# Sixteen small tiles instead of four in the products with P and dS of a recurrent attention kernel

## The chip, the cores and the metric

The kernel runs on one core of a Trainium2 chip. The metric is device time of one execution in microseconds. A core has TensorE (PE, matrix products, with its weight loads shown apart as PEld), VectorE (DVE), ScalarE (ACT), GpSimd (POOL) and SyncE (SP, which issues most transfers). PE writes into PSUM, eight banks of 2 KB in each of 128 partitions, from where DVE and ACT copy ("evict") results to SBUF. A matmul can be placed on a part of the 128x128 array: `tile_position=(r, c)` puts it on the rows from r and the columns from c. Its rows are the partitions that it reads, its columns the PSUM partitions that it writes.

## The reference

A training step, forward and backward, of a layer with two branches over 2048 tokens of width 512: `x + A(xn) + B(xn)`, with xn the layer norm of x. Branch B is a squared-ReLU MLP. Branch A goes through 64 segments of 32 tokens, with 32 heads of width 128 and 8 memory rows:

```python
for s in range(n_seg):
    h = jnp.concatenate([mem, xs], axis=1)          # 8 + 32 rows
    q = jnp.einsum('btd,dhe->bhte', h, Wq)          # and k, v
    p = _softmax(where(mask, scores, -1e9))
    o = einsum(einsum(p, v), Wo)
    mem = o[:, :M, :]                               # goes into the next segment
...
_out, _vjp = jax.vjp(_f, A_x, A_mem0, A_Wq, ...)
```

Outputs are the layer's output and the gradients of all inputs and weights. The memory rows make the segments a serial chain, forward in one direction and backward in the other.

## The kernel before

The program has four stages. The first (0 to about 250 us) is the layer norm and branch B. The second is the forward recurrence (to about 1300 us), the third the backward recurrence (to about 2515 us), the last accumulates the weight gradients of branch A and the layer norm's gradient.

In both recurrences one segment is one call of `chain(s)`, and four segments make a block of 128 tokens. The 32 heads lie in 4 groups of 32 partitions by 8 slots: tile [128, 8, 128], partition group j, slot i, head 4i + j. A projection (`proj`, lines 407 to 421) puts four heads' columns on four column groups of the array at once and evicts in two halves of four slots. `to_T` transposes 128x128 pieces on PE.

In the forward, `chain` (line 907) does q and k, their transposes, scores, softmax on DVE and ACT, transposes P in 32x32 squares on DVE, and then `diag` (line 441) multiplies P with V for each head: out (32 x 128) = P (32 x 32 or 32 x 8, the weights) times V (32 x 128), two terms (own rows and memory rows). As a head's P and V lie in partition group j and its output shall lie there as well, `diag` uses the four tiles on the diagonal of the array, tile_position (32j, 32j), one half of four slots into one PSUM bank, 32 matmuls a half. Each half is evicted with its own copy of 128x512 (`evict`), transposed on DVE in 32x32 squares (`sq_T`, 128x512) and multiplied with Wo (`wo_part`, line 814), 128 matmuls, whose result gives the next segment's memory.

In the backward, `chain` (line 1236) does the projection gO, its transposes gOT, dP = gO V^T (line 1249), the softmax's gradient on DVE (`smax_bwd`, lines 1101 to 1106, four operations), which gives dS, and three `diag` products: part 2 (P with gO), part 1 (dS with q) and part 0 (dS transposed with k). Each is evicted, transposed by `sq_T` and goes through `dh_part` (line 1117, 64 matmuls of 512 columns) into one PSUM bank. That bank is copied to R_A, summed over the groups (gm, line 1284) and written into the next segment's input (line 1287).

Other blocks' work fills the gaps: in the forward the weight gradients of branch B (`dw_unit`, line 1009) and the four memory-row sets of a block in one go (`l_proj`, `l_attn`, names with L); in the backward `l_pre` and `l_post`, with an own `diag` each (oL and dqL), and in `l_post` two products `own` (line 1194) and `mm` (line 1205) that add up in one bank per half.

The order is made by a planner (`_Plan`): every piece of work is added with a cost in us for the engines that can do it, with what it reads and writes. `run()` simulates with these costs and issues the pieces in the order found, so that each engine's queue has a fixed order. PE work has a shape ("d" for diag, "w" for column groups, "f" for the whole array), and a turn between shapes costs 0.095 us in the plan.

PSUM banks come from pools of the tile framework. In the forward kinds c, f and m have 4, 2 and 2 banks (`NBK`), in the backward c, r and f have 5, 1 and 2. `Stage.bank` gives the banks of a kind in turn.

## Time and profile before

| | us |
|---|---|
| median of 3 runs | 3122.26 (3120.48 to 3124.76) |
| profiled execution: span | 3097.7 |
| PE busy in the span | 2792.6 |
| DVE busy | 1538.8 |
| ACT busy | 933.7 |
| forward recurrence, one segment (250 to 1300, 64 segments) | 16.4 |
| backward recurrence, one segment (1369 to 2515) | 17.9 |

The span is counted from the first to the last instruction of the profiled execution. The runs time the whole execution: their median is 24.6 us above the span. In the lines of the profile, "x" counts instructions, "idle before" is the time in which an engine stood still ahead of an instruction, and the name behind the arrow is what ended it. "issue" stands for time in which the engine waited for nothing that the profile shows. Busy time of PE is modelled and counts overlapping matmuls once.

### The profile page before, as it was taken

Reading aid. Unit: us, or ns where it says so; the run is one execution under the profiler, and the core shown is the slowest. Engines: PE = TensorE matmul, PEld = TensorE weight load, DVE = VectorE, ACT = ScalarE, POOL = GpSimd, SP = SyncE. Lnnn points to the kernel's source line nnn. Section 1 sums busy time; section 2 is a strip of 40 time slices with the busy share of each in tenths; the row PEclk is TensorE's granted clock in tenths of the full one; section 3 lists DMA queues with packets and bytes.
Section 4 is the critical chain, followed back from the end, with each engine's and each line's share of the span. In section 5 each row is a group of like instructions: output and inputs, shape, how many; then the busy total and the mean of one; then the engine's idle time right before and its main releaser. Section 6 shows DMA issues by size and latency. Waiting matters only on the chain.

```text
span 3097.7 us, 138545 instructions
## 1 busy us (share of the span) xinstructions
PE 2792.6 (90%) x62681; PEld 1629.5 (53%) x62847; DVE 1538.8 (50%) x3390; ACT 933.7 (30%) x1809; POOL 260.8 (8%) x434
## 2 busy tenths in 40 slices
PE   8998889898889898798888898889899889999999
PEld 6664555555555555564555555555555544444444
DVE  5544545555545455575555565565556521233322
ACT  4323434433434344342233333333333310000000
POOL 1110000000000000100000000000000001121111
PEclk9999999999999999999999999999999989999999
DMA  6647655566665563357677777777777669789861
GB/s 205 217 155 212 173 157 171 160 174 167 163 160 153 162 168 125 98 143 195 184 208 193 204 204 202 207 200 213 208 214 206 201 238 351 223 253 280 253 184 45
DMA packets 554918, 590.54 MB, mean 191 GB/s; under 512 B 250197, under 2 KB 355110, under 8 KB 552150
## 3 DMA queue, kind: packets, MB, share of 16 engines
q1 hardware_dynamic: 538758, 527.06, 59.8%
q0 software_dynamic: 15568, 54.61, 5.3%
q8 instruction: 491, 8.04, 1.2%
q14 instruction: 101, 0.83, 0.1%
HBM read 283.32 MB, written 262.68 MB: 176 GB/s over the span
## 4 chain that ended last, share of the span: by engine, by line
PE 67%; issue 10%; DVE 8%; DMA 8%; SPq 3%; ACT 2%; POOL 1%; ACTq 0%; POOLq 0%; DVEq 0%
PE ps_gw L1448 11%; PE ps_dRA L1117 9%; PE ps_d L451 6%; PE ps_RA L814 4%; PE ps_q L415 4%; PE ps_k L415 3%; PE ps_h L609 3%; PE ps_gO L415 3%; SPq L361 3%; PE ps_dRL L1117 3%; PE ps_v L415 2%; PE ps_dw L1009 2%; PE ps_gm L1284 2%; PE ps_o L451 2%; PE ps_gxb L637 2%
## 5 line engine op out<-in xcount | busy, mean ns | idle before, releaser
L1117 PE MATMUL ps_dRA<-WA,dT 128*32 128x512 bf16 x6144 | 376.6, 385 | 12.9 <-issue 10.4
L1448 PE MATMUL ps_gw<-WA,WB 128*128 128x512 bf16 x1505 | 330.7, 379 | 2.2 <-DVE gwo L316 0.6
L415 PEld LDWEIGHTS <-PA 128*32 128x32 bf16 x8192 | 207.5, 98 | 235.7 <-issue 29.8
L1448 PEld LDWEIGHTS <-WB 128*128 128x128 bf16 x1896 | 185.4, 98 | 225.0 <-issue 1.9
L399 DVE STREAM_TRANSPOSE dT<-dN 128x512 bf16<-128x512 bf16 x384 | 255.5, 692 | 90.7 <-ACT dN L318 89.4
L318 ACT CAST dN<-ps_d 128x512 bf16<-128x512 f32 x356 | 198.8, 588 | 292.0 <-PE ps_d L451 257.2
L1117 PEld LDWEIGHTS <-dT 128*32 128x32 bf16 x6144 | 158.0, 97 | 169.5 <-issue 26.5
L316 DVE CAST gwo<-ps_gw 128x512 bf16<-128x512 f32 x64 | 39.7, 683 | 399.5 <-PE ps_gw L1448 268.2
L814 PE MATMUL ps_RA<-WB,OT 128*32 128x128 bf16 x8192 | 139.3, 223 | 58.2 <-issue 41.9
L318 ACT CAST gwo<-ps_gw 128x512 bf16<-128x512 f32 x64 | 32.9, 599 | 515.3 <-PE ps_gw L1448 357.8
L316 DVE CAST kN<-ps_k 128x512 bf16<-128x512 f32 x117 | 80.9, 691 | 191.4 <-PE ps_k L415 188.4
L415 PE MATMUL ps_q<-WA,PA 128*32 128x512 bf16 x2048 | 160.9, 383 | 9.5 <-DVE PA L951 5.5
L814 PEld LDWEIGHTS <-OT 128*32 128x32 bf16 x8192 | 123.4, 99 | 78.9 <-issue 48.2
L415 PE MATMUL ps_k<-WA,PA 128*32 128x512 bf16 x2048 | 159.7, 380 | 1.6 <-issue 1.3
L451 PEld LDWEIGHTS <-PB 32*32 32x32 bf16 x8192 | 120.4, 93 | 72.6 <-issue 33.9
L415 PE MATMUL ps_gO<-WB,PA 128*32 128x512 bf16 x2048 | 139.5, 418 | 15.1 <-DVE PA L1287 14.9
L1227 POOL COPY bVT<-VR 128x1024 bf16<-128x1024 bf16 x64 | 66.6, 1041 | 959.1 <-PE ps_dP L1249 880.8
L318 ACT CAST qN<-ps_q 128x512 bf16<-128x512 f32 x119 | 69.6, 585 | 197.8 <-PE ps_q L415 194.7
L415 PE MATMUL ps_v<-WA,PA 128*32 128x512 bf16 x2048 | 128.1, 378 | 0.0
L1009 PE MATMUL ps_dw<-sx,anT 128*128 128x512 bf16 x358 | 108.0, 385 | 10.3 <-DMA sx<-in_grad_out_dram 6.6
L399 DVE STREAM_TRANSPOSE OT<-oN 128x512 bf16<-128x512 bf16 x128 | 83.8, 691 | 59.6 <-ACT oN L318 59.0
L1117 PE MATMUL ps_dRL<-WA,LT 128*32 128x512 bf16 x1536 | 111.2, 395 | 1.4 <-issue 1.0
(298 smaller groups left out, 4778.2 us busy)
## 6 DMA issues: line engine op xcount, KB each, us to landing
S_GN<-dN SPq DMA_DIRECT2D x192, 256.0 KB
WA<-S_GN SPq DMA_DIRECT2D x160, 256.0 KB
S_Q<-qN SPq DMA_DIRECT2D x64, 256.0 KB
S_K<-kN SPq DMA_DIRECT2D x64, 256.0 KB
S_V<-vN SPq DMA_DIRECT2D x64, 256.0 KB
S_ON<-oN SPq DMA_DIRECT2D x64, 256.0 KB
bqN<-S_Q SPq DMA_DIRECT2D x64, 256.0 KB
bkN<-S_K SPq DMA_DIRECT2D x64, 256.0 KB
```

Source lines behind the costliest of these rows:

```text
L316: nc.vector.tensor_copy(out, in_)
L318: nc.scalar.copy(out, in_)
L361: self.plan.add({eng: cost}, lambda e: q.dma_start(out_f(), in_f()), R, W, prio, lat)
L399: self.plan.add({"DVE": 0.70}, lambda e, x=x: nc.vector.transpose(dst[:, x, :, :], src[:, x, :].rearrange("p i (a c) -> p i c a", c=JQ)), ...
L415: nc.tensor.matmul(bk()[32 * j:32 * (j + 1), :], lhsT=win(dc), rhs=Wt(dc, c0), start=(dc == 0), stop=(dc == DC - 1), tile_position=(0, 32 ...
L451: nc.tensor.matmul(bk()[32 * j:32 * j + m, k * P:(k + 1) * P], lhsT=lf(j, i), rhs=rf(j, i), start=(k == 0 and x == 0), stop=(x == n - 1), ...
L609: nc.tensor.matmul(bk()[:, x, :], lhsT=Wt[:, dc, fc * P:(fc + 1) * P], rhs=In[:, dc, :], start=(dc == 0), stop=(dc == DC - 1), skip_group_ ...
L814: nc.tensor.matmul(bk()[32 * jd:32 * (jd + 1), :], lhsT=OTt[:, i, j, :], rhs=Wo[:, JQ * i + j, jd * P:(jd + 1) * P], start=(i == 0 and j = ...
L1009: nc.tensor.matmul(bks[x]()[:], lhsT=anT[x][:, c, :], rhs=sx[z][:], start=(c == 0), stop=(c == TC - 1))
L1117: nc.tensor.matmul(bk()[32 * j:32 * (j + 1), :], lhsT=XT[:, i, j, :], rhs=wtf(t, JQ * i + j), start=(first and i == 0), stop=(last and i = ...
L1227: A({"POOL": 1.0}, lambda e: nc.gpsimd.tensor_copy(VT[:, :, :, M:KA].rearrange("p i j r -> p (i j) r"), VR[:].rearrange("p i j r -> p (i j ...
L1448: nc.tensor.matmul(bks[n]()[:], lhsT=HNc[:, rc, dc * P:(dc + 1) * P], rhs=gns[y][:, hf * 512:(hf + 1) * 512], start=(y == 0), stop=(y == N ...
```

## The change

`diag` uses all sixteen 32x32 tiles of the array. A head still comes from partition group r, but its product goes to column group c, another number: the 32 heads are dealt so that head 16x + 4r + c is read from rows r and written to columns c. Matmuls from row group r write PSUM bank r of four, at columns 128x, so that a result has slot 2r + x in partition group c. One `diag` of kind c takes the banks 0 to 3 at once, is one piece of 64 matmuls in the plan (before: two of 32), and is evicted by two copies of two banks (256 columns of each) after it. Of kind f, which has two banks, two row groups go at a time; the second two wait for the eviction of the first. `own` and `mm` of `l_post` are split by row groups instead of by slots in the same way.

PSUM in the two recurrences is one tile of eight banks; a bank of a kind is a view of it with a key ("ps", number). In the backward the count of kind c starts at 0 in each segment, so that gO has banks 0 and 1, gOT 2 and 3, dP 4, and the three products 0 to 3.

As the heads of a result are dealt in another order than before, the weights are taken in the matching order: `wf` and `wof` read 512 contiguous columns or four neighbouring heads for a half, `wo_part` and `dh_part` go through the heads by `hs`, `turn` writes two runs of 512, and the last stage reads its rows through `half_of` and writes out_6 by `hs`.

```diff
+class _View:
+    def __call__(self):
...
+        t = self.ps[0:self.shape[0], self.key[1], :]
...
+            if self.ps is not None:
+                return _View(self.ps, ("ps", self.pools[key[0]][0] + key[1]), shape, dt)
...
         def turn(self, kind, nm, reg, key, okey):
-                dc, i0 = g % DC, 2 * (g // DC)
-                blk = reg[:, dc, i0 * JQ * P:(i0 + 2) * JQ * P]
+                blk = reg[:, g % DC, :].rearrange("p (x r f) -> p r x f", x=2, r=JQ)[:, g // DC]
...
+        def quad(self, kind):
+            b = self.pools[kind][0]
+            return [(b, b + 1), (b + 2, b + 3)] if kind == "c" else [(b, b + 1)] * 2
+
         def diag(self, kind, nm, terms, rkeys, dst, prio):
             n = len(terms)
-            for half in range(2):
-                bk = self.bank(kind, [P, 512], F32, "ps_" + nm)
-
-                def mm(e, half=half, bk=bk):
-                    for k in range(4):
-                        i = 4 * half + k
-                        for x, (lf, rf, m) in enumerate(terms):
-                            for j in range(JQ):
+            pairs = self.quad(kind)
+            def mms(rows):
+                for x in range(2):
+                    for y, (lf, rf, m) in enumerate(terms):
+                        for d in range(JQ):
+                            for r in rows:
+                                c = (r + d) % JQ
+                                i = JQ * x + c
                                 nc.tensor.matmul(
-                                    bk()[32 * j:32 * j + m, k * P:(k + 1) * P], lhsT=lf(j, i), rhs=rf(j, i),
-                                    start=(k == 0 and x == 0), stop=(x == n - 1), tile_position=(32 * j, 32 * j),
-                                    skip_group_check=True,
+                                    self.ps[32 * c:32 * c + m, pairs[r // 2][r % 2], x * P:(x + 1) * P],
+                                    lhsT=lf(r, i), rhs=rf(r, i), start=(x == 0 and y == 0), stop=(y == n - 1),
+                                    tile_position=(32 * r, 32 * c), skip_group_check=True,
                                 )
-                self.plan.add(pe(0.23 * n, "d"), mm, rkeys(half), [bk.key], prio)
-                self.evict(lambda half=half: dst[1][:, 4 * half:4 * half + 4, :].rearrange("p i e -> p (i e)"),
-                           bk, lambda bk=bk: bk()[:], [(dst[0], half)], prio, EV_F)
+            if kind == "c":
+                self.plan.add(pe(0.13 * n, "d"), lambda e: mms(range(JQ)), rk, keys(0) + keys(1), prio)
+            for g in range(2):
+                if kind != "c":
+                    self.plan.add(pe(0.115 * n, "d"), lambda e, g=g: mms((2 * g, 2 * g + 1)), rk, keys(g), prio)
+                self.evict_quad(pairs[g], g, dst, prio)
+
+        def evict_quad(self, pair, g, dst, prio):
+            self.plan.add(EV_F, lambda e: ev(
+                {"DVE": "v", "ACT": "s"}[e], dst[1][:, 4 * g:4 * g + 4, :].rearrange("p (r x) e -> p r (x e)", x=2),
+                self.ps[:, pair[0]:pair[0] + 2, 0:2 * P]), [("ps", k) for k in pair], [(dst[0], g)], prio)
...
+    def slot4(c0):
+        return JQ * (c0 % HW // 512) + c0 // HW
+    def hs(s):
+        return JQ * (s % 2) + s // 2
     def wf(t):
-        w = Wqkv[t].rearrange("p c (i j e) -> p c i j e", i=NI, j=JQ)
-        return lambda dc, c0: w[:, dc, c0 % HW // P:c0 % HW // P + 4, c0 // HW, :]
+        return lambda dc, c0: Wqkv[t][:, dc, slot4(c0) * JQ * P:(slot4(c0) + 1) * JQ * P]
...
-        sg = Stage(plan, {"c": (pc, NBK[0]), "f": (pc, NBK[1]), "m": (pc, NBK[2])})
+        sg = Stage(plan, {"c": (0, 4), "f": (4, 2), "m": (6, 2)}, pc.tile([P, 8, 512], F32, name="ps"))
...
-                                    rhs=Wo[:, JQ * i + j, jd * P:(jd + 1) * P],
+                                    rhs=Wo[:, JQ * hs(i) + j, jd * P:(jd + 1) * P],
...
-        sg = Stage(plan, {"c": (pc, 5), "r": (pc, 1), "f": (pc, 2)})
+        sg = Stage(plan, {"c": (0, 5), "r": (5, 1), "f": (6, 2)}, pc.tile([P, 8, 512], F32, name="ps"))
...
-                                             rhs=wtf(t, JQ * i + j), start=(first and i == 0),
+                                             rhs=wtf(t, JQ * hs(i) + j), start=(first and i == 0),
...
+                pairs = sg.quad("f")
+                for g in range(2):
...
+                    A(pe(0.12, "d"), own, lk, bkeys)
...
+                    A(pe(0.27, "w"), mm, rk, bkeys)
+                    sg.evict_quad(pairs[g], g, ("dLN", dLN), 1)
...
+            sg.cnt["c"] = 0
             sg.proj("c", "gO", win, [("gT", p), ("gm", p, v), "WB"], wof, 0, ("gN", gN), 0)
...
-            bk = sg.bank("c", [P, NI, KA], F32, "ps_dP")
+            bk = sg.bank("f" if sg.rings else "c", [P, NI, KA], F32, "ps_dP")
...
+        def half_of(t, x):
+            return t.rearrange("p (r x e) -> p x r e", r=JQ, x=2)[:, x]
...
-                                             rhs=gns[y][:, hf * 512:(hf + 1) * 512],
+                                             rhs=half_of(gns[y], hf),
...
-                        nc.gpsimd.dma_start(out_6[JQ * k + j], wt[:])
+                        nc.gpsimd.dma_start(out_6[JQ * hs(k) + j], wt[:])
```

## The prediction

> **What bounds the kernel now.** I read the page first, for the engines' shares and the chain of work that ended last.
>
> ```profile
> span 3097.7 us, 138545 instructions
> PE 2792.6 (90%) x62681; PEld 1629.5 (53%) x62847; DVE 1538.8 (50%) x3390; ACT 933.7 (30%) x1809; POOL 260.8 (8%) x434
> ...
> q8 instruction: 491, 8.04, 1.2%
> ...
> PE 67%; issue 10%; DVE 8%; DMA 8%; SPq 3%; ACT 2%; POOL 1%; ACTq 0%; POOLq 0%; DVEq 0%
> PE ps_gw L1448 11%; PE ps_dRA L1117 9%; PE ps_d L451 6%; PE ps_RA L814 4%; PE ps_q L415 4%; PE ps_k L415 3%; PE ps_h L609 3%; PE ps_gO L415 3%; SPq L361 3%; PE ps_dRL L1117 3%; PE ps_v L415 2%; PE ps_dw L1009 2%; PE ps_gm L1284 2%; PE ps_o L451 2%; PE ps_gxb L637 2%
> ```
>
> TensorE leads, and the products that change (line 451) hold 6% and 2% of the chain, some 250 us. Only the forward and backward recurrences contain them, so next I took the table of stretches: PE, weight loads, DVE, ACT, POOL busy, clock, DMA share, GB/s.
>
> ```profile
> 250.00:1300.00 1050.00, 915.40 (x27397) 561.07 (x27486) 541.54 (x1219) 415.78 (x805) 26.51 (x48) 0.99 0.57 158
> 1369.00:2515.00 1146.00, 1018.84 (x29114) 608.63 (x29118) 660.49 (x1316) 360.53 (x667) 89.85 (x138) 0.96 0.73 201
> ```
>
> Over 64 segments a forward one takes 16.4 us with 14.3 of PE, a backward one 17.9 with 15.9. PE is nearly full, but beside a serial chain whose gaps other blocks' work fills. The timeline of one undisturbed backward segment (1906.9 to 1922.8, 15.9 us) shows where the changed products sit.
>
> ```profile
> 1909.33 0.40 PE L312 MATMUL ps_gOT<-ident,gON 128*128 128x128 bf16 x4
> 1909.66 0.23 PE L451 MATMUL ps_d<-gON,bP 32*32 32x128 bf16 x4
> 1909.73 0.23 PE L451 MATMUL ps_d<-gLN,bPLL 32*8 32x128 bf16 x4
> 1909.78 0.22 PE L451 MATMUL ps_d<-gON,bP 32*32 32x128 bf16 x4
> ...
> 1910.22 0.40 PE L312 MATMUL ps_gOT<-ident,gON 128*128 128x128 bf16 x4
> ...
> 1914.11 0.23 PE L451 MATMUL ps_d<-bqN,maskA 32*32 32x128 bf16 x4
> ...
> 1914.79 1.07 ACT L318 CAST dN<-ps_d 128x512 bf16<-128x512 f32 x2 [2.77 <-DVE PB L1266]
> ...
> 1915.41 1.31 DVE L399 STREAM_TRANSPOSE dT<-dN 128x512 bf16<-128x512 bf16 x2 [0.32 <-ACT dN L318]
> ...
> 1917.09 3.64 PE L1117 MATMUL ps_dRA<-WA,dT 128*32 128x512 bf16 x64
> ```
>
> Four matmuls start together, then the next four 55 ns later: a product (64 matmuls, two halves of 32) takes 16 such rounds, 0.89 us, or 14 ns per load-and-matmul pair. A half is evicted while the other is computed. The last view is a dense place in the forward.
>
> ```profile
> 782.84 1.17 PE L814 MATMUL ps_RL<-WB,qLT 128*32 128x128 bf16 x69 [0.20 <-issue]
> 783.80 1.01 PE L814 MATMUL ps_RA<-WB,OT 128*32 128x128 bf16 x59
> 786.32 1.17 PE L814 MATMUL ps_RA<-WB,OT 128*32 128x128 bf16 x69 [1.51 <-issue]
> 787.28 0.65 PE L814 MATMUL ps_RL<-WB,qLT 128*32 128x128 bf16 x32
> ```
>
> Between two such halts, 69 + 59 = 128 matmuls and their loads ran: 256 instructions. The 491 instruction packets of the page, for 125,528 PE instructions, are 256 each, and in the trace no two start less than 3.3 us apart. PE therefore stops when it spends 256 instructions in less than about 3.4 us (here 782.84 to 786.32, 3.5 us). That limit does not change; the new products spend instructions faster.
>
> **The change, part by part.**
>
> *PE time of the serial products.* There are 64 in the forward and 192 in the backward. Sixteen tiles at once would take 4 rounds of 55 ns, 0.22 us, plus start. The trace shows no sixteen at once. Its bounds are 14 ns per pair (four tiles, as now: no gain) and 3.4 ns (the pace at which the four pairs inside a round are issued, 12 to 14 ns for four). I take 4 ns, 0.26 us, because two rows are near it: the row groups run side by side in these products, and the four column groups do in line 1117, whose 64 matmuls of 512 columns take 3.64 us, 228 ns for four. A gain below zero is not excluded by any row, and I leave it to the rivals. At 0.26, 256 x 0.63 = 161 us of PE time go.
>
> The Trainium skill, TensorEngine Tiling (Array Packing), Key Properties, says that tiles load and multiply independently, sixteen of them at 32x32. By that rule the term would be 256 x 0.67 = 172 us; the trace agrees as far as four.
>
> *Background products.* 32 (oL and dqL) run 8 tiles, two banks at a time, in 0.45 instead of 0.89: 14 us. The 32 own products of l_post go from 0.44 to 0.22: 7 us. Group 1 now waits on PE for group 0's eviction (ACT 0.58 or DVE 0.69, plus 0.2), as both use the same bank pair. What queues behind is whatever the planner puts there, and LT and oL come up to 1 us later. They have a block of some 70 us to be done in; if that cover is short, it costs 4 x 1 us per block, 64 us, against nothing. I take nothing.
>
> *What of it the forward's chain gets.* Now the first half is computed in 0.45, evicted in 0.58, transposed in 0.69 (DVE), and line 814 starts. Afterwards all 0.26 must be done, then ACT and DVE evict side by side or ACT twice; the first transpose starts 0.45 - 0.26 = 0.2 us earlier, the second likewise, as two DVE transposes follow the first eviction either way. The other 0.44 is PE time for filler, which now sometimes delays the chain. But line 814 issues its 256 instructions in 1.8 us right behind, and its row has 41.9 us of issue halts: less time ahead of it lengthens these. Between nothing and 0.63 I take 0.3: 64 x 0.3 = 19 us.
>
> *What the backward's chain gets.* Three effects. (a) The product with gN stood between the two gOT transposes and between the two dP halves, 0.56 each with its switch. It now needs banks 0 to 3, and gOT lies in 2 and 3, so it waits for both gOT evictions; dP needs the same evictions and its bank is 4, so dP can go first. The softmax then starts about 0.5 us earlier. In return the first part's transpose falls into or behind the 2.1 us of softmax on DVE, and PE has only filler there. (b) After dS, the two products' 2 x 0.63 go from the PE sequence that runs without a gap from 1914.1 to 1920.7. (c) The last product waits on PE for both evictions of the one before it, since it uses the same banks: product end + 0.2 + 1.07 (two on ACT) is about 1915.2 to 1915.8 in this segment's times, against 1916.09 now. Line 1117's remaining matmuls fill that time and queue behind it. From there six DVE transposes of 0.69, with 1.0 us of smaller ones, last 5.2 us after dS and end about 1.0 to 1.4 us ahead of today's PE end. So 0.5 + 1.2 = 1.7 us, less the issue halts: two products and the matmuls between them are some 300 instructions in 1.9 us instead of 3.0, which by the 3.4 us rule adds 0.3 to 0.8. I take 1.2 us, between 0 and 2.2: 64 x 1.2 = 77 us.
>
> *Evictions.* Their number and size stay (128x512, 585 ns on ACT, 692 on DVE); one now reads two banks of 256 columns. I count that as nothing, since the bytes are the same; a per-bank restart would show as longer rows, and DVE's 50% covers it.
>
> *Banks and waits.* The pools become one tile of eight banks, with the same number of banks for each kind. Waits that go by bank cost nothing; see the rivals.
>
> *Weight order.* Projections read 512 contiguous columns instead of four runs of 128; the last stage's k, q, v gradients read four runs instead of 512. Strided (ps_q, 383 ns; ps_dRA, 385) and contiguous (ps_gw, 379) rows differ by 1%: nothing. The 48 evictions of the transposed Wq, Wk and Wv write two runs of 512 instead of 1024 elements: nothing, or at most 48 x 0.1 us either way. No DMA is added, dropped or resized; SP's and POOL's queues issue the same transfers at another pace, DMA share 0.73 rising to about 0.78.
>
> *Sum.* 19 + 77 = 96 us off the span of 3097.7, 3002. The median of the runs, 3122.26, is 24.6 above that span, which I take as what lies around it, unchanged: 3026 us.
>
> **Rivals.**
>
> 1. *The whole PE time counts*, because filler always waits for PE (for: 90% busy; against: the chain's DVE and ACT steps). 161 + 14 + 7 = 182 us, 2940; some dense places keep it above, so 2935 to 2985.
>
> 2. *Most is given back* by issue halts, by evictions that no longer overlap the product, and by DVE's queue, which stops behind late DMAs (4.78 us idle before one transpose at 1885.05, and the next gO took 3.60 us instead of 1.90). Forward nothing, backward 0.5: 32 us, 3090 (3060 to 3115). The Trainium skill, same page, PSUM Bottleneck, says the copy out of PSUM may bound after tiling; 1.07 us of ACT against 0.26 of product agrees with it.
>
> 3. *Slower: tiles of one row group in different column groups take turns.* The pace stays 14 ns, and nothing is evicted until the whole 0.89 is done: +0.45 in the forward, and in the backward +0.45 for each of the two products after dS, less the 0.5 of (a), plus 0.4 for the wait (c): 64 x (0.45 + 0.85) = 83 us, 3205. Against it stands line 1117. Between 4 ns (-96) and 14 ns (+83) the sign turns at about 9 ns per pair, 0.6 us per product.
>
> 4. *Waits go by the whole PSUM tile*, not by bank, so that PE stops for every eviction: some ten a segment, 0.6 us each, 128 segments, +770 us. Nothing in this trace can show it.
>
> **How the numbers follow.** Forecast 0.54 (3026, 2985 to 3060), rival 1 0.16, rival 2 0.14, rival 3 0.12, rival 4 0.02, no change within 0.2% (about what a measurement can tell from none) 0.02. Faster 0.84, same 0.02, slower 0.14. The range from 2935 to 3115 leaves out rivals 3 and 4, the rest of no change, and a little at each end.
>
> **What would show it.** Right: rounds of sixteen starts within 60 ns in the timeline and about 0.26 us per product; backward segments of about 14.5 us; more issue idle before lines 451, 814 and 1117. Wrong: rounds of four (rival 3); diag rows short but segments of 15.4 us with PE's share well under 85% (rival 2), or PE's share still at 90% with segments under 14 (rival 1); DVE or PE idle that ends on an eviction of another bank (rival 4). The prediction also fails if the planner's new order lets l_post's loads come late more often than now.

## The result and the profile after

The changed kernel takes 3210.95 us (median of four runs, 3202.69 to 3215.35), the kernel before beside it 3121.37. The ratio on record is 1.0312, 95% interval 1.0282 to 1.0342; like the other ratios below it is not the quotient of the two medians, which is 1.0287 here. The kernel is 3% slower, where 3026 us and faster had been forecast.

The page of the changed kernel, its span, busy shares, granted clock by fortieths, instruction packets and chain:

```profile
span 3200.9 us, 138721 instructions
PE 2784.4 (87%) x62723; PEld 1531.9 (48%) x62847; DVE 1617.9 (51%) x3506; ACT 861.5 (27%) x1693; POOL 259.6 (8%) x434
...
PEclk9999999999999999889889898889998899999999
...
q8 instruction: 491, 8.04, 1.1%
...
PE 13%; issue 5%; DMA 2%; DVE 1%; POOL 1%; SPq 0%; ACT 0%; POOLq 0%; DVEq 0%; ACTq 0%
```

PE's busy time fell by 8 us, where by rival 1 the shorter products were to save 182, and its granted clock is lower in the second half of the program. The chain that could be followed back covers only some 22% of the span here, so it is not used below. The stretches of the two recurrences (columns as before the change: PE, weight loads, DVE, ACT, POOL, clock, DMA share, GB/s):

```profile
258.00:1302.00 1044.00, 905.27 (x27146) 536.09 (x27229) 574.91 (x1256) 379.14 (x739) 22.23 (x42) 0.96 0.56 157
1387.00:2606.00 1219.00, 995.61 (x28652) 524.90 (x28652) 687.14 (x1358) 315.36 (x597) 89.84 (x138) 0.91 0.69 186
```

The loss is in the backward recurrence, 1219 us where the kernel before had 1146. From the write of one segment's gradient of the memory (PA, line 1287 before and 1332 now) to the next, a segment takes 16.84 us in the forward (before 16.74) and 19.66 in the backward (before 18.26): 62 x 1.40 = 87 us. These are single profiled executions. How far two of them can differ is seen in a run further down: e11 has the same forward program as the kernel before, and took 17.07 us a forward segment where that took 16.74. So the difference in the forward means nothing; that in the backward is four times as large as this.

The loss lies behind dS. From PA to dS it is 7.7 us in both, from dS to the last matmul of the chain's line 1158 (1117 before) 9.45 us for 7.95. In the same recurrence PE's idle time that ended on DVE is 110 us for 54, that on ACT 61 for 18, and that called "issue" 43 for 41. The timeline of one backward segment (start, duration, then what the engine waited for) shows both what the change does and where it loses. Line 478 is `diag` now, 1147 the last operation of the softmax's gradient (it writes dS), 421 `sq_T`, 1310 to 1312 the copy and the two transposes of dS that part 0 needs, 1158 `dh_part`.

```profile
1881.09 0.27 PE L478 MATMUL ps<-gON,bP 32*32 32x128 bf16 x16
1881.16 0.32 PE L478 MATMUL ps<-gLN,bPLL 32*8 32x128 bf16 x16
1881.34 0.35 PE L478 MATMUL ps<-gON,bP 32*32 32x128 bf16 x16
1881.48 0.34 PE L478 MATMUL ps<-gLN,bPLL 32*8 32x128 bf16 x16
1881.74 1.48 PE L437 MATMUL ps<-WB,PB 128*32 128x512 bf16 x24
...
1882.83 0.49 DVE L1147 SCALAR_TENSOR_TENSOR maskA<-btA,bP 128x320 bf16<-128x320 f32 x1
1883.24 1.30 DVE L421 STREAM_TRANSPOSE dT<-dN 128x512 bf16<-128x512 bf16 x2
1883.37 0.26 PE L478 MATMUL ps<-bqN,maskA 32*32 32x128 bf16 x11 [0.15 <-DVE maskA L1147]
1884.40 0.24 PE L478 MATMUL ps<-bqN,maskA 32*32 32x128 bf16 x5 [0.76 <-issue]
...
1885.14 1.07 ACT L338 CAST dN<-ps 128x512 bf16<-128x512 f32 x2 [1.19 <-issue]
1885.29 2.77 PE L1158 MATMUL ps<-WA,dT 128*32 128x512 bf16 x48
1885.76 0.71 DVE L421 STREAM_TRANSPOSE dT<-dN 128x512 bf16<-128x512 bf16 x1 [1.23 <-ACT dN L338]
1886.40 0.14 DVE L1310 COPY dSp<-maskA 128x64 bf16<-128x64 bf16 x1
1886.45 0.43 DVE L1311 STREAM_TRANSPOSE PB<-maskA 128x256 bf16<-128x256 bf16 x1
1886.81 0.40 DVE L1312 STREAM_TRANSPOSE PB<-dSp 128x256 bf16<-128x256 bf16 x1
1887.99 0.27 PE L478 MATMUL ps<-bkN,PB 32*32 32x128 bf16 x16
```

First, the sixteen tiles do run side by side, but not for long. The product with gO starts at 1881.09, and the next work of PE 0.65 us later; the same measure is 1.00 us in the kernel before. In an undisturbed product the first 32 pairs start within 0.12 us; then comes a gap of 0.13 us, and from there on a pair starts every 8.3 ns.

Second, dS is ready at 1883.3, but DVE takes its transposes only at 1886.4. Ahead of them in DVE's queue stands the transpose of part 1's result (1885.76), which waits 1.23 us for the eviction of a product that was itself halted for 0.76 us. Part 0, which needs these transposes and is last in the segment, starts 4.7 us after dS. It comes behind more than them: when they end, at 1887.2, PE is still busy with 48 matmuls of line 1158 (a product has 32, not 64), and the last 16 of these need part 1's transpose. In all 62 segments of the changed kernel one of part 1's transposes stands ahead of the last one of dS, in the kernel before in none.

Third, halts ("issue") fall into the product behind dS.

### The profile page after: what moved, and what is told of

Its sections match the earlier page's. It is cut to its first block, busy times and chain, and to the rows that moved or that the text cites. A ratio compares the mean times of both kernels' runs of the same rounds, so it can differ in the third digit from the quotient of the medians.

```text
span 3200.9 us, 138721 instructions
## 1 busy us (share of the span) xinstructions
PE 2784.4 (87%) x62723; PEld 1531.9 (48%) x62847; DVE 1617.9 (51%) x3506; ACT 861.5 (27%) x1693; POOL 259.6 (8%) x434
## 5 line engine op out<-in xcount | busy, mean ns | idle before, releaser
L1158 PE MATMUL ps<-WA,dT 128*32 128x512 bf16 x6144 | 427.8, 423 | 32.2 <-DVE dT L421 17.4
L437 PE MATMUL ps<-WA,PA 128*32 128x512 bf16 x6144 | 376.0, 388 | 11.5 <-issue 6.2
L1497 PE MATMUL ps<-WA,WB 128*128 128x512 bf16 x1536 | 332.3, 379 | 0.6 <-DVE gwo L336 0.6
L338 ACT CAST dN<-ps 128x512 bf16<-128x512 f32 x286 | 158.3, 587 | 412.5 <-issue 298.6
L855 PE MATMUL ps<-WB,OT 128*32 128x128 bf16 x8192 | 147.8, 231 | 48.1 <-issue 29.3
L437 PE MATMUL ps<-WB,PA 128*32 128x512 bf16 x2048 | 145.2, 432 | 37.5 <-DVE PA L1332 37.5
L1158 PE MATMUL ps<-WA,LT 128*32 128x512 bf16 x1536 | 113.5, 397 | 17.9 <-ACT dLN L338 13.2
L1050 PE MATMUL ps<-sx,anT 128*128 128x512 bf16 x360 | 105.5, 383 | 15.2 <-DMA sx<-in_grad_out_dram 8.2
L437 PE MATMUL ps<-WA,PB 128*32 128x512 bf16 x1536 | 104.1, 383 | 8.8 <-ACT KT L338 4.3
L1501 PE MATMUL ps<-GOc,WA 128*128 128x512 bf16 x486 | 106.9, 379 | 0.5
```

Source lines behind the costliest of these rows:

```text
L338: nc.scalar.copy(out, in_)
L437: nc.tensor.matmul(bk()[32 * j:32 * (j + 1), :], lhsT=win(dc), rhs=Wt(dc, c0), start=(dc == 0), stop=(dc == DC - 1), tile_position=(0, 32 ...
L855: nc.tensor.matmul(bk()[32 * jd:32 * (jd + 1), :], lhsT=OTt[:, i, j, :], rhs=Wo[:, JQ * hs(i) + j, jd * P:(jd + 1) * P], start=(i == 0 and ...
L1050: nc.tensor.matmul(bks[x]()[:], lhsT=anT[x][:, c, :], rhs=sx[z][:], start=(c == 0), stop=(c == TC - 1))
L1158: nc.tensor.matmul(bk()[32 * j:32 * (j + 1), :], lhsT=XT[:, i, j, :], rhs=wtf(t, JQ * hs(i) + j), start=(first and i == 0), stop=(last and ...
L1497: nc.tensor.matmul(bks[n]()[:], lhsT=HNc[:, rc, dc * P:(dc + 1) * P], rhs=half_of(gns[y], hf), start=(y == 0), stop=(y == NRC - 1))
```

## The experiments

Each was run beside the kernel before, on the same chip as it. This table holds means over 62 backward segments of one profiled execution each, in us, worked out from the starts and ends of the instructions named. Part 0's own matmuls lie between the third and the fourth of these columns: the third counts to its first matmul, the fourth from its last. The half clock is the time with a granted clock of 0.5 between 1320 and 2640 us. The halts are stops of PE of over 0.2 us, between the first and the last PA of both recurrences, that end 1.2 to 1.5 us after an instruction packet has landed, added up (on the reason for this, see the runs on instructions).

| kernel | ratio to before | segment | dS to the end of its transposes | dS to the first matmul of part 0 | last matmul of part 0 to the last of line 1158 | half clock | halts |
|---|---|---|---|---|---|---|---|
| before | 1 | 18.26 | 1.69 | 3.03 | 3.64 | 99 | 87 |
| changed | 1.0312 | 19.66 | 3.30 | 5.20 | 3.80 | 229 | 94 |
| e1_small_first | 1.0067 | 18.50 | 1.97 | 4.56 | 4.11 | 191 | 106 |
| e13_order_kept_four | 1.0136 | 18.47 | 1.95 | 4.45 | 3.77 | 151 | 93 |
| e6_part2_early | 1.0012 | 18.38 | 1.36 | 2.82 | 4.61 | 202 | 90 |
| e10_fewer_instr | 0.9768 | 17.08 | 1.38 | 2.19 | 4.52 | 150 | 51 |

### DVE's order, and the plan that made it

The first theory was that the order on DVE makes the loss; its rival that the halts or the late evictions do. Three kernels: e1 is the changed one with part 1's transpose held behind those of dS, e2 the changed one with another price for a product in the plan (0.56 us for 0.26), e3 the kernel before with too low a price. The diffs in this order:

```diff
-        def sq_T(self, src, sk, dst, dk, prio):
+        def sq_T(self, src, sk, dst, dk, prio, R=()):
-                    [(sk, half)], [(dk, half)], prio)
+                    [(sk, half)] + list(R), [(dk, half)], prio)
...
-                sg.sq_T(dN[t], "dN%d" % t, dT[t], "dT%d" % t, 0)
+                sg.sq_T(dN[t], "dN%d" % t, dT[t], "dT%d" % t, 0, ["dSTA", "dSTL"] if t in (1,) else ())
```

```diff
-                self.plan.add(pe(0.13 * n, "d"), lambda e: mms(range(JQ)), rk, keys(0) + keys(1), prio)
+                self.plan.add(pe(0.28 * n, "d"), lambda e: mms(range(JQ)), rk, keys(0) + keys(1), prio)
```

```diff
-                self.plan.add(pe(0.23 * n, "d"), mm, rkeys(half), [bk.key], prio)
+                self.plan.add(pe(0.065 * n, "d"), mm, rkeys(half), [bk.key], prio)
```

> The changed kernel, with one thing more: part 1's DVE transposes also read the two small transposes of dS (dSTA, dSTL), so these stand ahead of them in DVE's queue. Theory Q (DVE's queue order: in the changed kernel a transpose that waits for part 1's eviction stands ahead of dSTA and dSTL, and part 0's product waits 5.20 us after dS instead of 3.03): dS to part 0 falls to about 3.3 us, the backward segment by about 1.9, and the run takes about 3090 us (3060 to 3130). Theory H (PE's halts for instructions and the half clock are the loss, whatever the order): above 3180 us.

> The changed kernel, with the plan's cost of a product of kind c set from 0.13 to 0.28 us a term, near the 0.55 us that the trace shows for two terms. Nothing else. Theory Q, with the plan's too small cost as the reason of the order: the plan puts dSTA and dSTL first again, and the run takes about 3090 us (3060 to 3130), as the first run of this call. Theory H: above 3180 us.

> The kernel before, with four tiles, two evicted halves and its own banks, but with the plan's cost of a half set from 0.23 to 0.065 us a term, so that the plan believes what it believes in the changed kernel. Theory Q: the plan alone makes it slower, by 1 us or more a backward segment, about 3190 us (3160 to 3230). Theory H, or the new waits for banks as the cause: within 20 us of the kernel before.

Measured: e1 3129.33 us, 1.0067 (1.0045 to 1.0089); e2 3147.08, 1.0111 (1.0078 to 1.0145); e3 3184.5, 1.0235 (1.0202 to 1.0268). DVE's part of the timeline in e1:

```profile
1912.73 0.49 DVE L1147 SCALAR_TENSOR_TENSOR maskA<-btA,bP 128x320 bf16<-128x320 f32 x1
...
1913.14 1.30 DVE L421 STREAM_TRANSPOSE dT<-dN 128x512 bf16<-128x512 bf16 x2
...
1914.36 0.14 DVE L1310 COPY dSp<-maskA 128x64 bf16<-128x64 bf16 x1
1914.41 0.43 DVE L1311 STREAM_TRANSPOSE PB<-maskA 128x256 bf16<-128x256 bf16 x1
...
1914.77 0.40 DVE L1312 STREAM_TRANSPOSE PB<-dSp 128x256 bf16<-128x256 bf16 x1
...
1915.89 1.30 DVE L421 STREAM_TRANSPOSE dT<-dN 128x512 bf16<-128x512 bf16 x2 [0.71 <-ACT dN L338]
```

The wait for part 1's eviction is still there, but behind the transposes of dS, which end 1.97 us after dS. The edit takes 1.0312 - 1.0067 = 2.45% back, 76 us of the 97. That is not the price of one transpose alone. The added dependence had the whole plan made anew, and other work moved with it: of the 1.16 us that a segment gets shorter, 0.64 lie ahead of dS, as the softmax starts 4.58 us after PA for 5.46. Behind dS the transposes end 1.33 us sooner, but part 0 starts only 0.64 sooner (4.56), where 3.3 had been expected. The order comes from the plan: with a product at 0.26 us, it had a transpose of part 1 first. In e2, with the product at 0.56 us and the same matmuls, part 1's transposes come behind those of dS in all segments, and 2.0% come back, 62 us, though 3147 us lies outside what either theory gave. And e3 shows the same without any new product: on the kernel before, the low price alone put a transpose of part 1 ahead of dS's (3.45 us from dS to their end) and cost 2.35%. Of the 89 us by which its profiled execution is longer, some 55 are in the backward recurrence and 33 in the forward, where no dS is. So the plan's order is shown as the cause of most of the loss; what the transposes of dS have of it, apart from what moved with them, is not.

### What sixteen tiles are worth

The loop over the diagonals is taken outermost, so that only four tiles are in use at a time. In e5 the plan's prices were raised with it, in e13 nothing else was changed against e1, so that every queue has the same order and only the matmuls inside a product are sorted differently.

```diff
-                for x in range(2):
-                    for y, (lf, rf, m) in enumerate(terms):
-                        for d in range(JQ):
+                for d in range(JQ):
+                    for x in range(2):
+                        for y, (lf, rf, m) in enumerate(terms):
```

> The changed kernel with its banks, evictions and dealing of heads, but the loop over d outermost, so that four tiles run at a time as before (0.89 us a product), and the plan's costs set to that (0.45 a term, 0.225 of kind f). Against the second run it tells what the sixteen tiles at once are worth, against the kernel before what the new banks and later evictions cost. Theory Q: 0.35 us a product on the path, three a backward and one a forward segment, so 60 us above the second run, about 3150 us (3120 to 3190). If the tiles' pace is worth nothing on the path: equal to the second run within 15 us.

> The kernel with DVE's order mended (part 1's transpose behind those of dS), every queue and every piece in the same order, the planner's costs as they were; only the 64 matmuls inside one product come in another order, the loop over d outermost, so that four tiles on one diagonal are used to the end before the next four (about 14 ns a pair, 0.9 to 1.05 us a product, for 8.3 ns and 0.55). It measures what the sixteen tiles alone are worth. If a product's length counts as it is: 0.4 us x (1 forward + 2 backward after dS) x 64 = 77 us slower than the mended kernel's 1.0067, plus a little for the product with gN: 3190 to 3215 beside 3110. If the time saved by sixteen tiles is mostly given back, because the same 256-instruction packets are waited for either way: 3140 to 3160.

Measured: e5 3233.63 us, 1.0399 (1.0369 to 1.0428); e13 3143.69, 1.0136 (1.0105 to 1.0167). By e5 alone the sixteen tiles would look worth 3% and more. But its plan had also put evictions ahead of dS's transposes, which ended 3.02 us after dS, so it measured an order once more. With the order kept, e13 against e1, sixteen tiles are worth 0.7%, 21 us (about 10 to 33 by the two intervals). This is less than the 77 that I expected, for two reasons. An undisturbed product in e13 takes 0.80 us to PE's next work, not 0.9 to 1.05: its 33rd pair starts after 0.25 us as with sixteen tiles, and only the rest go slower, at 13 ns a pair. So sixteen tiles save 0.15 us of a product, 256 x 0.15 = 38 us of PE. And part of that may be given back: halts go from 93 to 106 us, half clock from 151 to 191. Where the gain lies, the profiled executions don't tell: the forward segment is 16.72 against 16.87 us, the backward one 18.50 and 18.47, and both differences are within those of one program.

e13 also shows that the new form without the benefit of sixteen tiles, and with DVE's order mended, is 1.4% slower than the kernel before, although its products are shorter (0.80 for 1.00).

### Part 2 ahead of the softmax

In the kernel before, part 2 is computed in halves between the gOT transposes and dP, and in most segments the first of its two transposes on DVE comes ahead of dS. Now part 2 comes after dP, and both transposes, with the matmuls of line 1158 that need them, fall behind dS. In e6 part 2 is split into two groups of two banks, and the softmax waits for the first half of its transposed result; in e7 all three products, and the forward's, are split, and the softmax doesn't wait. The diff of e6 on top of e1:

```diff
-            if kind == "c":
+            if kind == "c" and not split:
...
-                if kind != "c":
-                    self.plan.add(pe(0.115 * n, "d"), lambda e, g=g: mms((2 * g, 2 * g + 1)), rk, keys(g), prio)
+                if kind != "c" or split:
+                    self.plan.add(pe(0.14 * n, "d"), lambda e, g=g: mms((2 * g, 2 * g + 1)), rk, keys(g), prio)
...
-              [bk.key, pkey], [k("bt")], prio)
+              [bk.key, pkey] + list(R), [k("bt")], prio)
...
-                sg.diag("c", "d%d" % t, terms, rk, ("dN%d" % t, dN[t]), 0)
+                sg.diag("c", "d%d" % t, terms, rk, ("dN%d" % t, dN[t]), 0, t in (2,))
...
-            smax_bwd("A", bk, KA, Pt[z], ("Pt", z), dS, "dS", 0, 0.51)
+            smax_bwd("A", bk, KA, Pt[z], ("Pt", z), dS, "dS", 0, 0.51, [("dT2", 0)])
```

> The first run's kernel (small transposes first), with part 2's product split again into two groups of row groups with two banks each, and the softmax's gradient made to wait for the first of part 2's DVE transposes, so that PE and DVE have the order of the kernel before: part 2's first 16 matmuls of line 1117 run during the softmax's gradient. Theory C (clock: in the changed kernel PE stands idle during the softmax's gradient, the clock is halved just after dS, and the products after it run at half pace): the time under half clock in the backward falls from 191 us to about 100, and the run takes about 3085 us (3060 to 3110), faster than the kernel before. Theory H (halts for instructions alone keep the rest): no better than 3115 us.

> The first run's kernel with every product of kind c split into two groups of two row groups and two banks, eight tiles at a time, each group evicted as soon as it is done (plan cost 0.14 a term and group). As the trace shows 8.3 ns a pair after the first 16 pairs whatever the tiles, eight tiles cost PE about the same, and the first half's eviction runs beside the second half. Theory E (evicting only after all 64 matmuls, and waiting for all four banks, is what eats the gain): 3095 us (3070 to 3115). Theory C: the idle during the softmax's gradient stays, so within 20 us of the first run, 3130 us.

Measured: e6 3109.48 us, 1.0012 (0.9991 to 1.0032); e7 3139.78, 1.0104 (1.0063 to 1.0145). Part 2's place, with the plan that it makes, is worth about 0.55%, 17 us, and brings the kernel level with the one before, not ahead. Theory C's half clock was to fall to about 100 us; it is 202, so the level time does not speak for it. Evicting each half early (e7) gains nothing against e1, so nothing says that the late evictions were what was missing. Its products, eight tiles at a time, take 0.68 us to PE's next work, hardly more than with sixteen. In e6 part 0 starts 2.82 us after dS, earlier than before the change (3.03), but from its last matmul to the last of line 1158 it takes 4.61 us for 3.64. A share of this is the clock. The group of line 1158 in the list of groups (busy us and mean ns, then idle before them), changed kernel, then e6:

```profile
L1158 PE MATMUL ps<-WA,dT 128*32 128x512 bf16 x6144 | 427.8, 423 | 32.2 <-DVE dT L421 17.4 <-issue 11.8 <-DVE brL L1144 2.7
```

```profile
L1158 PE MATMUL ps<-WA,dT 128*32 128x512 bf16 x6144 | 430.6, 421 | 33.9 <-DVE dT L421 18.8 <-issue 13.6 <-DVE PB L1312 0.7
```

Before, the same 6144 matmuls took 376.6 us, 385 ns each. The 51 to 54 us more go with the longer time at a clock of 0.5 (229 and 202 us for 99).

### Clock and instructions

Two additions to e1, issued behind the softmax's gradient, whose results aren't used: four matmuls of 512 columns a segment (0.87 us of PE, eight instructions), and 64 pairs of 32 columns (128 instructions, 0.53 us at 8.3 ns a pair). The two in this order:

```diff
+                for _ in range(4):
+                    nc.tensor.matmul(sg.ps[:, 0, :], lhsT=ident[:], rhs=Wqkv[2][:, 0, 0:512], start=True, stop=True,
+                                     skip_group_check=True)
```

```diff
+                for x in range(4):
+                    for d in range(JQ):
+                        for r in range(JQ):
+                            c = (r + d) % JQ
+                            nc.tensor.matmul(sg.ps[32 * c:32 * (c + 1), r, 0:32], lhsT=q_(ident, r)[:, 0:32],
+                                             rhs=q_(ident, r)[:, 0:32], start=True, stop=True,
+                                             tile_position=(32 * r, 32 * c), skip_group_check=True)
```

> The first run's kernel with 4 matmuls of 512 columns (8 instructions, 0.87 us) added in each backward segment, into a bank that is free, between part 2's evictions and part 1's product, their result unused. Theory C: this work fills the idle of PE, half-clock stretches that begin within 2 us after dS fall from 25 to under 10, and the run gets 15 to 45 us faster than the first run, about 3100 us. If the clock is not the cause: 0 to 55 us slower than the first run.

> As the run before it in this call, but with 64 pairs of 32 columns on sixteen tiles (128 instructions, about 0.55 us) in place of the 4 long matmuls, their result unused. Theory H (PE's supply of instructions is used up at this place): 128 more instructions at 13.3 ns each cost up to 1.7 us a segment, 30 to 100 us more than with the 4 long matmuls, about 3160 us. If the supply is no limit: equal to or faster than with the 4 long ones.

Measured: e8 3145.86 us, 1.0127 (1.0104 to 1.0150); e9 3255.75, 1.0485 (1.0461 to 1.0510). e8 adds 64 x 0.87 = 56 us of PE work to e1 and costs 0.6%, 19 us; its half clock is 109 us for 191, and 10 stretches of it begin within 2 us behind dS where 25 did. So it gives back part of what it costs, but theory C's 15 to 45 us of gain did not come. e9 has less PE work than e8 and is 111 us slower, a little more than the upper end expected. Its halts are 169 us (e8: 112), and its half clock is 311. Both additions also wait for an eviction, as they write to banks of the products, 23 us in e8 and 33 in e9 between 1390 and 2420 us. The 128 instructions thus cost about 0.9 us a segment more than their time on PE and that wait; the trace doesn't part the halts from the half clock that comes with them.

How the two hang together is seen in one segment of e1. Its timeline on PE, from one halt to the next:

```profile
1914.53 0.23 PE L478 MATMUL ps<-bqN,maskA 32*32 32x128 bf16 x4 [0.43 <-issue]
1914.55 0.27 PE L478 MATMUL ps<-bqLN,dSL 32*8 32x128 bf16 x15
1914.61 0.23 PE L478 MATMUL ps<-bqN,maskA 32*32 32x128 bf16 x1
1914.61 0.21 PE L478 MATMUL ps<-bqLN,dSL 32*8 32x128 bf16 x1
1914.61 0.42 PE L478 MATMUL ps<-bqN,maskA 32*32 32x128 bf16 x15
...
1914.82 0.34 PE L478 MATMUL ps<-bqLN,dSL 32*8 32x128 bf16 x16
1915.09 0.62 PE L1158 MATMUL ps<-WA,LT 128*32 128x512 bf16 x8
...
1915.53 1.90 PE L1158 MATMUL ps<-WA,dT 128*32 128x512 bf16 x32
...
1917.36 0.28 PE L478 MATMUL ps<-bkN,PB 32*32 32x128 bf16 x16
1917.42 0.27 PE L478 MATMUL ps<-bkLN,PB 32*32 32x128 bf16 x16
1917.61 0.24 PE L478 MATMUL ps<-bkN,PB 32*32 32x128 bf16 x3
...
1920.67 0.27 PE L478 MATMUL ps<-bkN,PB 32*32 32x128 bf16 x13 [2.82 <-issue]
```

```profile
1917.61:1920.67 3.06, 0.24 (x26) 0.10 (x3) 0.00 (x0) 0.00 (x0) 0.00 (x0) 1.00 1.49 289
1921.86:1925.28 3.42, 3.42 (x40) 1.37 (x36) 1.28 (x3) 0.00 (x0) 0.00 (x0) 0.50 0.75 257
```

From 1914.53 on 4+15+1+1+15+16+8+32+16+16+3 = 127 matmuls run, with their loads 254 instructions; then PE stops in the middle of part 0, at the place on which the segment's end depends, for 2.82 us. In the trace an instruction packet starts at 1918.17 and has landed at 1919.28; PE goes on 1.39 us later. The packet before had landed at 1913.19, and that halt ended 1.34 us later. Over the recurrences of the changed kernel, 105 of 438 stops end 1.2 to 1.5 us after a landing, where chance would put some 25 (0.3 us of about 5 us between packets). The second line is what follows: 1.2 us after PE's return its clock falls to 0.5 for 3.41 us, in which a matmul of line 1158 starts every 97 ns, where it is every 46 just before and after (table of stretches; the columns are PE, loads, DVE, ACT, POOL, clock, DMA share, GB/s).

Why the clock falls there can be read from all the traces together. In each, its changes lie on a fixed grid of 3.413 us. From the first PA of the forward to the last of the backward, over all fourteen kernels, 606 stretches of that grid at full clock have PE busy for less than half; 534 of them are followed by one at a clock of 0.5. Of the 6779 with PE busy for 70% or more, 15 are. So neither one long stop nor a halt for instructions is needed: waits of any kind that leave PE idle for half of one stretch mostly come before a fall. That they cause it is borne out by e8, whose added work fills PE's idle time behind the softmax and takes the half clock from 191 to 109 us.

The Trainium skill, Runtime: NRT & Kernel Launch, Instruction fetch mechanics, states blocks of 256 instructions, and that crossing into the next is mostly hidden. The packets agree with the first (491 of them for 125,570 PE instructions); with the second the halts do not.

The Trainium skill, TensorE: Matmul & The Clock Gate, Part 1, states half speed after an idle window of some 3.4 us, and a return after as long a busy one. The stretch of 3.41 us agrees; the idle time does not, as PE stood still for 2.82 us here and half a stretch was mostly enough above.

### Fewer instructions

If the halts are for want of instructions, fewer of them in a segment must gain more than the time of the products left out. Parts 2 and 1 leave out their second term, that of the memory rows, in e6 and in the kernel before.

```diff
             part(2, [(lambda j, i: q_(Pt[z], j)[:, i, M:KA], lambda j, i: q_(gN, j)[:, i, :], 32),
-                     (lambda j, i: q_(PLL[p], j)[:, i, c0:c0 + M], lambda j, i: q_(gLN[p], j)[:, i, :], M)],
...
             part(1, [(lambda j, i: q_(dS, j)[:, i, M:KA], lambda j, i: q_(qN, j)[:, i, :], 32),
-                     (lambda j, i: q_(dSL[p], j)[:, i, c0:c0 + M], lambda j, i: q_(qLN[p], j)[:, i, :], M)],
```

> Part 2 early as in the kernel with the sum split in two, but parts 2 and 1 of every backward segment leave out the terms of the memory rows (so dv and dq-side sums lack them): 128 PE instructions of 32 columns fewer per segment, 64 segments. Two theories of what is left to gain. Supply of instructions: a packet of 256 PE instructions never starts under 3.3 us after the one before, 13 ns an instruction, and the segment waits for it; then 128 instructions fewer are worth 128 x 13 ns = 1.7 us of a segment at most and about half of that where something else ends the segment: 60 to 110 us off, 3000 to 3050 beside a kernel before of 3110. Length of the products only: at 8.3 ns a pair two products lose 32 pairs each, 0.27 us each, and part 2 lies beside softmax: 25 to 35 us off, 3075 to 3085.

> The kernel before with the same terms (memory rows of parts 2 and 1 of the backward segments) left out: the same 128 instructions fewer per segment. Each product loses half of its 0.89 us there, so 0.44 us twice in 64 segments, 56 us of PE time that is on the chain at least for part 1: both theories say 30 to 60 us off, 3050 to 3080. It is the measure for the run beside it: if the kernel with sixteen tiles gains more than this from the same omission, its PE was short of instructions rather than of time; if it gains less, of neither.

Measured: e10 3028.99 us, 0.9768 (0.9738 to 0.9799); e11 3059.18, 0.9846 (0.9818 to 0.9874). The kernel before gains 1.5%, 48 us, near the 56 of PE time left out. The one with sixteen tiles gains 1.0012 - 0.9768 = 2.4%, 76 us, although its two products lose only 2 x 64 x 0.27 = 35 us. The list of PE's waits between 1390 and 2420 us names the rest (us in all, times, longest), e6 and then e10:

```profile
PE ps L478 <- issue: 30.2, 25, 3.2
...
PE ps L1158 <- issue: 14.7, 17, 2.4
```

```profile
PE ps L1158 <- issue: 10.5, 14, 3.2
...
PE ps L478 <- issue: 5.4, 6, 2.7
```

Of 45 us of halts on these two lines 29 are gone, and of the halts behind packets in both recurrences 39 (90 to 51). 35 + 39 = 74 of the 76 us, but this sum is in part luck: the half clock fell too, from 202 to 150 us, and PE's waits for dS and for transposes rose by 31 us on the same two lines. In the kernel before, the halts behind packets went from 87 to 84 us. That hides what the omission did, as the forward, which has the same program in both, went from 49 to 58 by itself. In the backward, where the terms are left out, they fell from 38 to 26, against 55 to 24 with sixteen tiles. So instructions cost both kernels time, and the one with sixteen tiles more. How much more is not settled by the 76 and 48 us: e10 has nearly the order of e6, but in e11 the plan came out anew, with 45 us of PE's waits for transposes on line 1117, between 1390 and 2420 us, where there had been 2.

### A candidate

e6 with the forward product split as well, and a price of 0.28 in the plan for the unsplit products.

```diff
-                self.plan.add(pe(0.13 * n, "d"), lambda e: mms(range(JQ)), rk, keys(0) + keys(1), prio)
+                self.plan.add(pe(0.28 * n, "d"), lambda e: mms(range(JQ)), rk, keys(0) + keys(1), prio)
...
-            ], lambda h: ["PTA", "PTL", ("vN", h), ("vLN%d" % p, h)], ("oN", oN), 0)
+            ], lambda h: ["PTA", "PTL", ("vN", h), ("vLN%d" % p, h)], ("oN", oN), 0, True)
```

> The kernel with part 2 early, and in the forward segments too the product with P in two groups of two banks (each evicted when its own half is done), the planner's cost of the unsplit products at 0.28 for 0.13 a column unit. With all products split the forward segment came down from 16.84 to 16.54 us, 0.2 below the kernel before, so 62 x 0.2 = 12 us: 3095 (3080 to 3115) beside 3108 of the kernel before. If the forward gain there came from elsewhere than the split, no change: 3108.

Measured: 3105.55 us, 1.0012 (0.9991 to 1.0033), the same as e6 and not distinguishable from the kernel before. The 12 us expected did not show. The forward segment is 16.55 us (16.74 before) and the backward one 18.33 (18.26), differences that single executions of one program have too. No version was found that beats the kernel before and computes all of it.

## Why the prediction was wrong

**The step that failed** is the backward's (c): "six DVE transposes of 0.69, with 1.0 us of smaller ones, last 5.2 us after dS". It took DVE's order as given and asked only how long each piece lasts. But part 1's result now becomes ready later, all at once, while the plan, with 0.26 us for a product, expects it earlier. So a transpose that waits was put ahead of those of dS. They end 3.30 us after dS for 1.69, part 0 starts 2.2 us later, and from dS to the last matmul of line 1158 it is 9.45 us for 7.95, where the step had this end come earlier. That the plan's order makes most of the loss is shown by e2 (the price alone, 62 us), e1 (76 us) and, on the old products, e3; that it is these transposes and not what was moved along with them is shown only in part. The planner was named at the end as something that could go wrong, but for the loads of `l_post`; the price in the diff was read as a fact and not as an assumption that orders queues.

**PE time of the serial products** was mis-sized. 0.26 us is 4 ns a pair, taken from near the 3.4 ns between pairs inside a round of four. That pace holds for the first 32 pairs; with the gap and 8.3 ns a pair for the rest, 0.65 us go by until PE's next work, for 1.00 before. The gain is 0.35 us and not 0.63, 256 x 0.35 = 90 us for 161.

**Forward, 19 us**: nothing of it can be seen (16.84 for 16.74 us a segment). **(a), the softmax 0.5 us earlier**: not in the changed kernel, where from PA to the softmax's start 5.46 us go by as before (5.43); in e1 it came and was larger (4.58). But moving part 2 back also moved its work behind dS, which the step named ("falls into or behind the 2.1 us of softmax on DVE") and gave no price: 17 us by e6. **(b), shorter products behind dS**: 0.35 each for an undisturbed one, but the backward segment of e1 with sixteen tiles is no shorter than that of e13 with four.

**Halts**, 0.3 to 0.8 us a segment, were seen in kind, and the 256 instructions with them. In sum they are hardly more in the changed kernel (94 us for 87), and 19 us more in e1, 0.1 us a segment. What was missing is what follows when PE stands idle for half of a stretch, by them or by other waits: 3.4 us at half clock. The half clock (up from 99 to 229 us) was not in the sum at all; line 1158 alone is 51 us longer, which is a large part of why PE's busy time fell by 8 us and not by 90 and more.

**The 24.6 us** between span and median were taken as what lies around the span. The changed kernel's profiled execution took 3202.69 us with a span of 3200.9, so only 1.8 us lie around it; by the same 1.8 the execution profiled before the change took some 3099.5 us and was below its median. The forecast, 96 us off that median, stays the same.

**Evictions at nothing** held: two on ACT take 1.07 us as before. The background products and the strided weights were not measured by themselves.

**Rivals.** Rival 3's time (3205) is near the measured one, but its mechanism is not what happened: tiles of a row group don't take turns at 14 ns. Its turning point was nearly met, though: 0.6 us a product was to be the point of no gain, and the product takes 0.51 us to its last start. Rival 2 named issue halts and DVE's queue, rightly, but as a loss of gain only. Nothing like the 770 us of rival 4 came.

What stays open: why the new form with four tiles (e13) is 1.4% behind the kernel before although its products are shorter. Part 2's place explains some 17 of its 42 us. The rest may lie in the half clock (151 for 99 us) or in part 0's later start (4.45 us behind dS for 3.03), but no run separates the two.

## What to carry to other kernels

Where a planner's costs order the queues, a shorter piece of work changes the order too: look for what stands behind a waiting instruction on the other engines, and price the new piece by a measured one. An edit that is meant to move one transpose makes the plan anew, and its gain holds whatever else moved. Tiles of the PE array pay by the time of a whole product, not by the pace of its first round, and they don't lower the number of instructions; where PE halts for packets of them, leaving instructions out can be worth more than making them shorter. To measure one part of a change, keep every queue's order: e5 and e13 differ by 2.6% in a change of the same few lines.

## What the hardware showed

- A product of 64 load-and-matmul pairs on sixteen tiles: 32 pairs within 0.12 us, a gap of 0.13 us, then 8.3 ns a pair; with eight tiles at a time (e7) 9.2, with four (e13) 13.
- Packets of 256 PE instructions never start less than 3.2 us apart, some 13 ns an instruction, while a product on sixteen tiles spends one every 4.15 ns. In the changed kernel 105 stops of PE, four times as many as by chance, end 1.2 to 1.5 us after a packet's landing.
- The clock changes on a grid of 3.413 us. Of the stretches at full clock with PE busy for less than half, 534 of 606 are followed by one at 0.5; with PE busy for 70% or more, 15 of 6779. In e1, 25 of the 43 falls in the backward come within 2 us behind dS.
- 64 pairs of 32 columns, added in each of 64 segments (e9), cost 111 us more in all than four matmuls of 512 columns in the same place (e8).
